# Attention steps between the products of a block-matrix layer, and an earlier first input

## The chip, the cores and the metric

The kernel runs on one core of a Trainium2 chip. The metric is device time in microseconds (us) of one execution. The engines are named as in the profile: PE (TensorE, matrix products), ACT (ScalarE), DVE (VectorE), POOL (GpSimd) and SP (SyncE, which here only issues DMAs). Each engine executes its instructions in the order in which the program writes them; they meet through semaphores.

## The reference

An attention over 4 batches, 8 heads, 768 positions and head size 64 is followed by a mixture of 4 experts over the 3072 tokens that it yields.

```python
scores = scale * np.matmul(q, k.transpose(0, 1, 3, 2))
mask = np.where(retr[0, :, 0, 0, None, None], full_mask, stream_mask)
scores = np.where(mask[None, :, :, :], scores, -1000000000.0)
...
a = a / (np.sum(a, axis=-1, keepdims=True) + 1e-09)
return np.matmul(a, v).astype(np.float32)
...
p = domain_probs / (domain_probs.sum(-1, keepdims=True) + 1e-09)
for e in range(E):
    h = np.maximum(x @ w1[e], 0.0)
    out += p[:, e:e + 1] * (h @ w2[e])
```

Three heads ("retrieval": 0, 2 and 6) attend to all earlier positions. The other five ("window" heads) see the first 4 positions and the last 64. The rows of x are the heads' outputs side by side (512 wide); w1 is 512 x 1024 and w2 1024 x 512 for each expert.

## The kernel before, in words

**Two streams in one program.** The program does not start the second half after the first. It writes attention steps between steps of the expert layers. Attention is cut into 8 groups, one for each batch and half sequence (384 query rows, all heads); group g gives three tiles of 128 tokens, `xT[g]`. The expert layers are `moe_steps` (L1163): token tiles 0 to 2 together, expert by expert (`plain_steps`, L937), then tile 3 alone, expert by expert, then ten pairs of tiles (`pair_steps`, L1046).

**A pair.** For each expert, `scale_inputs` (L1017; the DVE operation is L1028) multiplies `xT` by the routing probabilities `pB` into one of two buffers `xs`. The first layer (PE L1059) makes 4 banks of 8 matmuls for an expert, 16 banks for a pair, each emptied by one Relu of ACT (L1068) into six blocks of `hA`. PE's banks come from `bank` (L98), which has four buffers `pA` in turn; attention scores (L627) take from the same four. The second layer of all four experts together is written as seven half-size block products (PE L1092) on sums of blocks, each of 16 matmuls in two halves. ACT copies (`keep`, L1110) and DVE additions (`add`, L1113) combine the products; sums of weight blocks are made once (`weight_sums`, and `last_weight_sum`, L927), sums of input blocks while the first layer runs (`input_sums`, L1032, on DVE L1036 and L919) and between the products (`fourth_sum`, L1122).

**Shared space.** The finished sums of tiles 0 to 3 lie in `hA` too (`acc_of`, L933): tile 0's where block 3 of the pairs lies. They are stored by SP (L992) at the end of the plain steps. The Relu that writes there must wait for the store.

**A window head.** Its keys are transposed by SP from `kSr` to `kS` (L255), once a group. Its score (L627: seven matmuls of 54 or 55 columns) goes through ACT's Exp (L645) and DVE's mask (L649); the values (L739) go to one of two buffers `pV`; ACT takes the reciprocal of the row sums as Ln (L757) and Exp (L767), and DVE scales into `xT` (L762), which releases the buffer. `later` (L895) puts that DVE operation into the program only after 1300 ns of planned time (`LAG`, L893), so other DVE work may stand ahead of it. In group 2 and later the heads follow in the order 0, 2, 6, 1, 3, 5, 7, 4, so five window heads end a group. Retrieval heads use L675 for the values.

**What sets the order.** Every step of `moe_steps` yields its planned duration and a share. The main loop (L1245) sums duration times share in `spent`, and writes attention steps while the group is behind its plan: `plan[a]` (L1207) gives the value of `spent` at which group a begins and ends, and `att_ns` the group's length. `require` (L1233) writes all that is left of a group that the next step reads. POOL's loads for the next group are written when a group begins (`loads`, L1188) and behind the values.

The lines that follow are those of the profile.

The softmax here doesn't subtract the row's maximum and nothing guards it: scores larger than these inputs give would overflow.

## Time and profile before

| | |
|---|---|
| median of 13 runs | 402.8 us (400.33 to 404.1) |
| the profiled execution, its own time | 400.92 us |
| its span, first to last instruction | 399.2 us |
| PE busy | 379.7 us (95%), 3814 matmuls |
| DVE, ACT, POOL busy | 219.2, 231.2, 138.9 us |
| mean granted PE clock | 0.991 |
| pair layer 1 on PE (L1059) | 156.2 us, 1280 matmuls |
| seven products on PE (L1092) | 76.4 + 58.4 us, 640 + 480 matmuls |
| window heads on PE, first and last of group 2 | 101.99 us, 121.04 us |

Busy PE time counts overlapping matmuls, each with a modelled end, so 95% does not say how much could be saved; the waits of PE do. A wait is the idle time just before an instruction, with the engine or DMA that ended it. A timeline line reads: start, duration, engine, source line, operation, what is written from what, sizes, how many, and in brackets the idle time before it. Times count from the first instruction.

### The profile page before, as it was taken

What the parts mean: (1) busy time and instruction counts of PE and PEld (TensorE: products, weight loads), DVE (VectorE), ACT (ScalarE), POOL (GpSimd) and SP (SyncE); (2) the same over time, 40 slices, a digit from 0 to 9 for tenths busy, and PEclk for the clock granted to TensorE, in tenths of its full rate; (3) what the DMA queues carried; (4) which work ended last, traced back from release to release, by engine and by line L of the source; (5) the groups of instructions that cost most, each with busy time, mean ns of one, the idle gap of its engine ahead of it and who ended that gap; (6) DMA issues with size and microseconds to landing.
All of it is one profiled execution on the core that took longest, in us unless ns stands there. A gap on an engine that the chain in (4) does not pass through costs nothing.

```text
span 399.2 us, 9362 instructions
## 1 busy us (share of the span) xinstructions
PE 379.7 (95%) x3814; PEld 314.5 (79%) x3814; DVE 219.2 (55%) x472; ACT 231.2 (58%) x476; POOL 138.9 (35%) x182
## 2 busy tenths in 40 slices
PE   8899999996798997999999999999999999999996
PEld 4755556574687896899988898899988898888885
DVE  7736787545364465565554465574643465454440
ACT  3754469462495587375684487476683585361641
POOL 8824734973436605731454016621200000000000
PEclk9999999998899999999999999999999999999999
DMA  9999999999999999994799659993790120110101
GB/s 163 162 208 195 188 166 163 166 113 139 221 162 151 157 104 173 144 170 84 74 170 146 105 89 134 190 186 32 72 195 15 55 59 7 53 54 2 54 0 54
DMA packets 167631, 47.67 MB, mean 119 GB/s; under 512 B 156492, under 2 KB 161316, under 8 KB 167588
## 3 DMA queue, kind: packets, MB, share of 16 engines
q0 software_dynamic: 102656, 20.98, 73.3%
q1 hardware_dynamic: 63332, 25.70, 32.5%
q8 instruction: 30, 0.49, 0.5%
q10 hardware_dynamic: 1600, 0.39, 0.5%
q14 instruction: 13, 0.11, 0.1%
HBM read 48.82 MB, written 6.34 MB: 138 GB/s over the span
## 4 chain that ended last, share of the span: by engine, by line
PE 56%; ACT 3%; DVE 1%; issue 1%; ACTq 0%
PE pO L1092 26%; PE pA L1059 25%; PE pA L627 3%; ACT hA L1068 1%; PE pV L675 1%; PE pV L739 1%; ACT rc L757 1%; DVE xT L762 1%; ACT es L645 0%; DVE hA L919 0%; ACT rc L767 0%; DVE es L649 0%; DVE hA L1036 0%; ACT o L1154 0%; ACTq L1154 0%
## 5 line engine op out<-in xcount | busy, mean ns | idle before, releaser
L1059 PE MATMUL pA<-xs,w1sb 128*128 128x256 f16 x1280 | 156.2, 276 | 2.6 <-DVE xs L1028 2.6
L1059 PEld LDWEIGHTS <-w1sb 128*128 128x128 f16 x1280 | 122.6, 99 | 18.2 <-issue 2.9
L1068 ACT ACTIVATE hA<-pA 128x512 f16<-128x512 f32 x160 | 94.8, 598 | 44.5 <-PE pA L1059 35.5
L1092 PEld LDWEIGHTS <-hA 128*128 128x128 f16 x1120 | 107.1, 98 | 12.8
L645 ACT ACTIVATE es<-pA 128x384 f16<-128x384 f32 (+2 forms) x122 | 60.2, 510 | 39.1 <-PE pA L627 37.0
L1092 PE MATMUL pO<-w2sb,hA 128*128 128x256 f16 x640 | 76.4, 273 | 0.0
L281 POOL DMA_DIRECT2D vS<-in_v_dram x30 | 29.3, 983 | 89.4 <-PE pV L739 88.8
L1092 PE MATMUL pO<-tsb,hA 128*128 128x256 f16 x480 | 58.4, 273 | 0.0
L1028 DVE TENSOR_TENSOR xs<-xT,pB 128x1024 f16<-128x1024 f16 (+1 forms) x52 | 49.5, 973 | 16.0 <-PE pA L1059 15.9
L919 DVE TENSOR_TENSOR hA<-hA 128x1024 f16<-128x1024 f16 (+1 forms) x80 | 41.9, 554 | 0.9
L233 POOL DMA_DIRECT2D kSr<-in_k_dram x30 | 29.6, 998 | 19.1 <-issue 9.6
L963 ACT ACTIVATE hA<-pA 128x384 f16<-128x384 f32 (+1 forms) x64 | 22.3, 386 | 18.9 <-PE pA L950 17.8
L950 PE MATMUL pA<-xT,w1sb 128*128 128x384 f16 (+1 forms) x256 | 31.7, 273 | 0.2
L649 DVE TENSOR_TENSOR es<-es,mC 128x256 f16<-128x256 f16 (+1 forms) x42 | 10.8, 258 | 38.1 <-ACT es L645 37.8
L1113 DVE TENSOR_TENSOR o<-pO,s 128x256 f32<-128x256 f32 x30 | 12.7, 425 | 34.3 <-PE pO L1092 23.2
L971 PE MATMUL pO<-w2sb,hA 128*128 128x512 f16 x128 | 30.5, 380 | 0.3 <-DMA w2sb<-in_moe_w_dram 0.3
L649 DVE TENSOR_TENSOR es<-es,mS 128x384 f16<-128x384 f16 (+1 forms) x40 | 13.8, 348 | 30.4 <-ACT es L645 30.3
L762 DVE TENSOR_TENSOR xT<-pV,rc 64x384 f16<-64x384 f32 x37 | 20.4, 554 | 12.7 <-ACT rc L767 10.4
L757 ACT ACTIVATE rc<-pV,eps 64x384 f32<-64x384 f32 x37 | 21.3, 575 | 10.1 <-PE pV L739 9.4
L1110 ACT COPY s<-pO 128x256 f32<-128x256 f32 x30 | 11.2, 372 | 27.3 <-PE pO L1092 25.7
L950 PEld LDWEIGHTS <-w1sb 128*128 128x128 f16 x256 | 19.3, 98 | 8.5 <-issue 0.7
L627 PE MATMUL pA<-qT,kR 128*128 128x384 f16 (+2 forms) x120 | 24.6, 280 | 1.1 <-ACT hA L963 0.4
(113 smaller groups left out, 337.0 us busy)
## 6 DMA issues: line engine op xcount, KB each, us to landing
pB<-p_rows SPq DMA_DIRECT2D x10, 512.0 KB
out_dram<-o SPq DMA_DIRECT2D x19, 256.0 KB
w1sb<-in_moe_w_dram POOLq DMA_DIRECT2D x8, 512.0 KB, 9.8
w2sb<-in_moe_w_dram POOLq DMA_DIRECT2D x4, 1024.0 KB, 13.5
kSr<-in_k_dram POOLq DMA_DIRECT2D x30, 112.0 KB, 6.0
vS<-in_v_dram POOLq DMA_DIRECT2D x30, 112.0 KB, 4.6
q<-in_q_dram POOLq DMA_DIRECT2D x18, 128.0 KB, 7.6
vR<-in_v_dram POOLq DMA_DIRECT2D x24, 48.0 KB, 5.2
```

What stands on the lines that cost most here:

```text
L233: gp.dma_start(out=kSr[:, :, SH.index(h), own(h)], in_=windows_of(k, b, h, c),)
L281: gp.dma_start(out=t[:, :, own_v(h)], in_=windows_of(v, b, h, c))
L627: nc.tensor.matmul(out=ps[:, o : o + nq], lhsT=key_tile(b, c, h, t), rhs=qTs[b, c][:, hp, q0 : q0 + nq], start=(n == 0 or not first), stop ...
L645: nc.scalar.activation(out=es[:, 0:cols], in_=ps[:, 0:cols], func=AF.Exp, scale=SC)
L757: nc.scalar.activation(out=rc[r, :], in_=ps[o, 0:CH], func=AF.Ln, bias=eps[o, :])
L919: nc.vector.tensor_tensor(out=out, in0=a, in1=b, op=ALU.subtract)
L950: nc.tensor.matmul(out=pss[ft][:, 0:cols_n], lhsT=w1sb[:, e * DMP + ct, ft * P : (ft + 1) * P], rhs=x[:, ct, :], start=(n == 0), stop=(n = ...
L971: nc.tensor.matmul(out=ps_o, lhsT=hs[:, ft, j * P : (j + 1) * P], rhs=w2sb[:, e * FTP + ft, :], start=(ft == 0), stop=(ft == FTP - 1),)
L1028: nc.vector.tensor_tensor(out=o, in0=xin, in1=pb.to_broadcast([P, DMP, n, P]), op=ALU.mult)
L1059: nc.tensor.matmul(out=ps[:, f * PC : (f + 1) * PC], lhsT=w1sb[:, e * DMP + ct, (f0 + f) * P : (f0 + f + 1) * P], rhs=xs[:, ct, :], start= ...
L1068: nc.scalar.activation(out=blocks[:, b0 : b0 + 2, k0 : k0 + 2, :].rearrange("p t f x -> p f t x"), in_=ps.rearrange("p (f t x) -> p f t x" ...
L1092: nc.tensor.matmul(out=ps, lhsT=a[:, k, :], rhs=b(k), start=(first and k == 0), stop=(k == KT - 1), skip_group_check=not first,)
```

## The change

Four things change.

- In `pair_steps` a step of the first layer now counts 0.5 and a half product 1.57 in `spent`; both counted 1.0. The shares of the plain steps (0.6 and 1.4), which held only for tiles 0 to 2, now hold for tile 3 as well, since the main loop uses every step's share. So attention is written mostly between the products.
- The first scaled inputs of the first pair are written behind expert 1 of tile 3, two experts earlier than before (E is 4).
- The last weight sum of expert 3 is not written behind tile 3, but behind the first bank of the first pair.
- Group 2 ends, and group 3 begins, at 0.72 of a pair instead of 0.66.

```diff
+    PSHARE = 1.57
+
     def pair_steps(nt0, nxt):

-        sums = []
+        sums = [lambda: last_weight_sum(E - 1)] if nt0 == pair0 else []
         for e in range(E):
...
                 if sums:
                     sums.pop(0)()
-                yield 2 * DMP * mm_ns(PC), 1.0
+                yield 2 * DMP * mm_ns(PC), 0.5
...
                 if k == KT // 2 - 1:
-                    yield KT // 2 * mm_ns(HN), 1.0
+                    yield KT // 2 * mm_ns(HN), PSHARE
...
         last = nxt is None
-        half = KT // 2 * mm_ns(HN), 1.0
+        half = KT // 2 * mm_ns(HN), PSHARE
...
             yield from plain_steps(3, 1, e, lambda: xT[1][:, :, 0:P], n0)
-            last_weight_sum(e)
-            if e == E - 1:
+            if e + 1 < E:
+                last_weight_sum(e)
+            if e == E - 3:
                 scale_inputs(pairs[0], 0)
...
-    for a, n in zip(range(2, G), (0.66, 1.65, 3.2, 4.65, 6.2, 7.65)):
+    for a, n in zip(range(2, G), (0.72, 1.65, 3.2, 4.65, 6.2, 7.65)):
...
     for ns, share in moe_steps():
-        spent += ns * (share if spent < E * UNIT else 1.0)
+        spent += ns * share
```

On PE the order of the instructions changes from tile 3 on; their number and kinds do not. On DVE the `scale_inputs` of the first pair and the weight sum move as told. On SP the four stores of tiles 0 to 3 now stand together, behind the key transpose of group 2 where three of them stood before, and the loads of `pB` shift by a place against the transposes of a few groups. The lines of the changed kernel are 3 or 4 higher than before from L1046 on: L1059 becomes L1062, L1068 L1071, L1092 L1095, L1110 L1113, L1113 L1116.

## The prediction

> **What bounds the kernel now.** Read first the list of waits, TensorE alone. From 60 us on PE waits four times only, 11.3 us together:

> ```profile
> PE pV L739 <- DVE xT L762: 5.4, 6, 2.2
> PE pA L627 <- DMA kS<-kSr: 2.9, 1, 2.9
> PE pA L1059 <- DVE xs L1028: 2.6, 1, 2.6
> PE pA L627 <- ACT hA L963: 0.4, 1, 0.4
> ```

> Elsewhere it streams: 8 matmuls of 256 columns take 0.87 us wherever the chain of waits shows them alone. No matmul is removed, so the change can win at most these 11.3 us. The last three waits are neighbours, and the timeline of 90 to 104 us shows what stands behind them. TensorE:

> ```profile
> 94.32 1.03 PE L1059 MATMUL pA<-xs,w1sb 128*128 128x256 f16 x8 [2.58 <-DVE xs L1028]
> ...
> 101.99 0.47 PE L627 MATMUL pA<-qT,kS 128*128 128x54 f16 x7 [2.94 <-DMA kS<-kSr]
> 102.28 1.89 PE L1059 MATMUL pA<-xs,w1sb 128*128 128x256 f16 x8
> ```

> ScalarE, idle in the same stretch, but not waiting for PE:

> ```profile
> 97.40 0.60 ACT L1068 ACTIVATE hA<-pA 128x512 f16<-128x512 f32 x1 [1.42 <-PE pA L1059]
> 97.89 0.38 ACT L645 ACTIVATE es<-pA 128x256 f16<-128x256 f32 x1
> 102.60 0.60 ACT L1068 ACTIVATE hA<-pA 128x512 f16<-128x512 f32 x1 [4.33 <-DMA out_dram<-hA]
> ```

> The third Relu of a pair writes blocks 2 and 3 of hA, where tile 0's finished sum lies (`acc_of`), so it waits for that sum's store. The store stands in SP's queue behind the transpose of the window keys:

> ```profile
> 90.44 8.47 SPq L255 DMA_TRANSPOSE kS<-kSr  x1
> 99.00 1.49 SPq L992 DMA_DIRECT2D out_dram<-hA  x3
> ```

> So two DMAs hold this place: kS at 101.99 and the store at 102.60. And the table of windows shows the clock (columns: stretch, us, busy time and count of five engines, granted PE clock, DMA share, GB/s):

> ```profile
> 91.80:95.20 3.40, 0.88 (x9) 0.79 (x9) 3.40 (x5) 0.00 (x0) 1.03 (x2) 1.00 1.72 121
> 95.20:98.60 3.40, 3.40 (x23) 2.46 (x21) 1.12 (x5) 1.47 (x3) 0.00 (x0) 0.51 1.44 174
> 98.60:102.10 3.50, 0.56 (x8) 0.22 (x6) 0.00 (x0) 0.00 (x0) 0.00 (x0) 0.99 1.40 231
> 102.10:105.50 3.40, 3.40 (x27) 2.59 (x26) 1.26 (x5) 1.58 (x3) 3.04 (x4) 0.50 1.20 285
> ```

> Each stretch in which PE idled is followed by one at half clock: the x8 of L1059 took 1.89 at 102.28.

> **Part 1, first scaled inputs earlier, group 2 begun later.** Two L1028 of 1.2 us each (2.35 for both) leave the place before L1059. The first now stands behind last_weight_sum(1), at about 85 us, the second among group 2's masks; the last weight sum (0.68) moves behind the pair's first bank, and its reader is only the fifth product. pB, issued at 69.53, has 15 us to land; were it late, DVE's masks and evictions would queue behind the L1028, under the cover described next. The 0.42 wait goes because that score now stands four layer-2 matmuls later. So PE starts layer 1 at 91.57, when L971 ends, not at 94.32.

> Now what is late next. I count PE work D from the pair's first layer-1 matmul, at full clock: 0.87 a bank, 0.18 for six L675 or seven 54-column matmuls, 0.11 for a 256-column score. Before, the kS score stands at D = 3 x 0.87 + 0.18 + 0.11 = 2.91. After, by the new order, layer 1 issues five banks, one L675 group and one score first: D = 5 x 0.87 + 0.29 = 4.66, reached at 91.57 + 4.66 = 96.23. The next bank, the pair's sixth, is the one that the third Relu must empty (`bank` has four, and a score took one between). Nothing that the change moves is ahead of the store on SP: the transpose waits for kSr's DMA and the store for the transpose's issue. So the Relu still starts at 102.60 and ends at 103.20, and PE restarts at about 103.25 at D = 4.66. The 2.58 and 2.94 are not saved; they become **one wait of 7.0 us**, named for L1068's counterpart or the store. Behind that Relu on ACT queue two Relus and an exponential, at a pitch of 0.5 against PE's 0.87 a bank; they catch up.

> Before, PE restarts at 101.99 with D = 2.91 and does half speed until 105.49: D = 2.91 + 3.50/2 = 4.66 there. After, at 105.49: 4.66 + 2.24/2 = 5.78 if the clock comes back then, 1.12 ahead. If it stays at half one stretch more, to 108.90, D is 4.66 + 5.65/2 = 7.49 against 4.66 + 3.41 = 8.07: 0.58 behind. Which? The stretch 102.07 to 105.49 would be 2.24/3.42 = 66% busy. Stretches that were 26% and 16% busy did not keep the clock, full ones did; at the start of the kernel, PE is busy from 1.27, and the slow matmuls last until about 6.5. 66% lies between, so I take the middle, **0.27 us gained**, ends +1.12 and -0.58.

> [...]

> **Part 2, attention between the products.** In layer 1 PE waits for nothing after 106 us, so fewer attention steps there win nothing. What may win is the tails of the groups, where five window heads A to E end a group. `pV` has two buffers, so C waits until A is scaled: 0.39 from A's L739 to its end, Ln 0.58, Exp 0.52, the L762 0.56, small gaps, 0.1 to PE: 2.3 us if no engine has other work. Rows:

> ```profile
> 121.43 0.58 ACT L757 ACTIVATE rc<-pV,eps 64x384 f32<-64x384 f32 x1 [0.84 <-PE pV L739]
> 122.04 0.52 ACT L767 ACTIVATE rc<-rc 64x384 f32<-64x384 f32 x1
> ```

> Before, the tails wait 2.04 (group 2, at 121.04), 2.23 (group 3, 155.20), 0.58 (group 5, 242 to 244) and 0.59 (group 7, 331 to 333). For after I walk each tail by the new order of ACT and DVE, counting from A's start.

> Group 2: A, B, C, D, E stand at 0, 2.11, 3.34, 4.39, 5.45 of PE work. DVE: the mask of the next score ends at 2.61, then the first add of the products (its product is ready at 2.31) 2.63 to 3.05, then A's scale to 3.63: C starts at 3.78, **0.44 late**. B's scale, behind one more mask, ends at 5.08: D at 5.23, 0.40 late. L919 (0.68) goes before C's scale, which ends at 6.35: E 0.21 late. Sum 1.05, so 0.99 gained.

> Group 3: 0, 1.24, 2.47, 3.53, 3.71, closer, because the planner is behind and issues two heads at once. The mask ahead of A's scale waits for an exponential that ACT does after A's Ln and Exp (2.03): A's scale ends 2.98, C 0.66 late. ACT: B's Ln and Exp to 3.17, a copy, an exponential to 4.08; DVE's mask to 4.45, B's scale to 5.03: D 0.99 late. C's scale to 5.80: E 0.59 late. Sum 2.24: nothing gained.

> Groups 5 and 7: 0, 1.23, 3.34, 4.39, 5.45 each, and A's scale stands ahead of the add. D 0.45 to 0.5 and E 0.15 late: 0.58 and 0.65, nothing gained. Groups 4 and 6 (2 to 3 us between heads) wait in neither kernel. Tails: **0.9 us gained**; each walk may err by 0.3.

> Other queues: group 3's key transpose starts after the last kS score of group 2 (about 119 us) and takes 6.3, first use at about 145; group 4's q transposes, now behind a pB load on SP, have about 7 us of slack; POOL's vS loads follow the values, which end within a microsecond of before. All hidden.

> **Sum.** 0.27 + 0.9 = 1.2 us. The profiled execution took 400.92 (span 399.2, 1.7 around it): 399.7 after. It lies 1.9 below the median of the 13 runs, 402.8, so by the same difference **401.6**, that is 0.29% faster. With the ends of the clock and the tails: 400.3 to 402.6.

> **Rivals.**
> - The store does not hold PE (it lands earlier, or a bank is free). Then PE stops at the kS score, D = 6.40, until 101.99, and its lead is 6.40 - 2.91 = 3.49; with the tails 4.4: **398.4**. For: it is what the new order of group 2 does if only PE's own waits counted. Against: the 4.33 row of ACT and the unchanged order on SP.
> - Slower: the scale operations in groups 5 and 7 are delayed as in group 3, 2.24 each. Place: pairs 4 and 7, second to fourth product. It decides once A's scale falls behind the mask that waits for the next exponential. Price 2 x 1.66 = 3.3: **404.9**; one group alone 403.2. For: the same 1.23 from A to B as in group 3. Against: in the order, A's scale is ahead.
> - The moves do what they say and are worth nothing: that is the lower end of my sum, 402.5.

> **Chances.** Forecast 0.72, store rival 0.13, slower rival 0.15. 0.3% (1.2 us) is about what a measurement of this kernel tells from no change. The forecast lies on that bound: 0.30 of its 0.72 is faster (clock back at once, 400.7), 0.40 the same, 0.02 slower. Faster 0.43, same 0.40, slower 0.17. Range 398.0 to 404.3, from the store rival to most of the slower one.

> **What would show it.** A wait of some 7 us of PE between 96 and 103, ACT's third Relu still released by out_dram at about 102.6, no wait for xs, half clock after 103; PE's waits for L762 near 4.5 in all, over 2 of it in group 3. If that Relu runs before 100, or the L762 waits pass 6, I am wrong.

## The result, and the profile after

The changed kernel takes **397.83 us** in the median of 11 runs (396.88 to 403.18), the kernel before 403.22 us in the median of 48 (398.61 to 404.47). The ratio is **0.9894, 95% interval 0.9864 to 0.9924**: 3.1 to 5.5 us faster, 4.3 in the middle (the plain medians lie 5.4 apart; the ratio, which has the interval, is used in what follows). The forecast was 401.6, a gain of 1.2. The measured median lies just under the range's lower end of 398.0; by the ratio, from the 402.8 that the forecast started from, it would be 398.5, just inside. The profiled execution took 397.6 us (span 395.9, against 399.2), so 3.3 us of the difference can be looked up in the two traces. PE is busy 378.4 us, in the same 3814 matmuls.

First the list of waits, TensorE alone (us in total, times, the longest). From 60 us on, only these two are left:

```profile
PE pA L1062 <- ACT hA L1071: 6.6, 1, 6.6
PE pV L739 <- DVE xT L762: 2.4, 6, 0.7
```

The waits for `xs` (2.6) and `kS` (2.9) are gone, and one wait of 6.6 us has come. PE's timeline shows its place:

```profile
95.14 0.27 PE L627 MATMUL pA<-qT,kR 128*128 128x256 f16 x1
102.01 3.57 PE L1062 MATMUL pA<-xs,w1sb 128*128 128x256 f16 x16 [6.60 <-ACT hA L1071]
105.38 0.53 PE L627 MATMUL pA<-qT,kS 128*128 128x54 f16 x7
105.73 2.92 PE L1062 MATMUL pA<-xs,w1sb 128*128 128x256 f16 x16
```

ScalarE's timeline, where the third Relu of the pair is the first of three, and the SP queue's:

```profile
101.36 1.57 ACT L1071 ACTIVATE hA<-pA 128x512 f16<-128x512 f32 x3 [8.23 <-DMA out_dram<-hA]
```

```profile
90.98 6.89 SPq L255 DMA_TRANSPOSE kS<-kSr  x1
97.97 2.01 SPq L992 DMA_DIRECT2D out_dram<-hA  x4
```

The store of tile 0's sum is issued behind the key transpose, the Relu waits for the store, and PE, with all four banks full, waits for the Relu. When the `kS` score comes, at 105.38, there is no wait for the keys any more. The 16 matmuls after the wait take 3.57 us, twice the usual 1.91, because the clock is at half for three stretches (columns as in the table of windows before):

```profile
97.57:100.98 3.41, 0.00 (x0) 0.00 (x0) 0.00 (x0) 0.00 (x0) 0.00 (x0) 0.50 1.37 263
100.98:104.39 3.41, 2.38 (x12) 1.65 (x12) 0.23 (x1) 2.33 (x5) 3.21 (x4) 0.50 1.05 252
104.39:107.81 3.42, 3.42 (x23) 2.49 (x22) 0.52 (x2) 1.26 (x4) 1.72 (x2) 0.50 1.84 156
```

PE works at half speed from 102.01 to 107.81, which costs 5.80/2 = 2.9 us; before, it was 1.75.

The tails of the groups. PE's timeline of `pV`, groups 2 and 3; groups 5 and 7 have one wait of 0.28 each:

```profile
122.27 0.35 PE L739 MATMUL pV<-es,vS 128*128 128x54 f16 x7 [0.37 <-DVE xT L762]
154.59 0.36 PE L739 MATMUL pV<-es,vS 128*128 128x54 f16 x7 [0.35 <-DVE xT L762]
156.53 0.36 PE L739 MATMUL pV<-es,vS 128*128 128x54 f16 x7 [0.72 <-DVE xT L762]
157.33 0.36 PE L739 MATMUL pV<-es,vS 128*128 128x54 f16 x7 [0.44 <-DVE xT L762]
```

**The account, profile against profile.** The tails cost 2.44 instead of 5.4: 3.0 gained. At the start of the pair, take the time at which PE restarts, add what the half clock costs after it, and subtract the work D that it had already done (D as in the prediction): before 101.99 + 1.75 - 2.91 = 100.83, after 102.01 + 2.90 - 4.66 = 100.25. That is 0.6 gained. But the Relu ran at 101.36 here and not at 102.60, since the key transpose's issue took 6.89 us instead of 8.47; with the store as late as before, and the clock as long at half after it, this place would have lost 0.7 (an estimate). Together 3.6, against 3.3 in the spans. (The 0.3 too many comes from the way the list measures a wait; measured from start to start, as told further down, the tails gain 2.7, and the sum is 3.3.)

So the tails pay, and the front turns two waits into one. That is theory T; its rival F says that the earlier first inputs pay. The runs below test it. The first four were timed beside the kernel before on one chip (median 403.36), the last four on another (403.12).

### The profile page after: what moved, and what is told of

Read it like the earlier page. It is cut to its first block, busy times and chain, and to the rows that moved or that the text cites. A ratio compares the mean times of both kernels' runs of the same rounds, so it can differ in the third digit from the quotient of the medians.

```text
span 395.9 us, 9358 instructions
## 1 busy us (share of the span) xinstructions
PE 378.4 (96%) x3814; PEld 314.0 (79%) x3814; DVE 219.2 (55%) x472; ACT 233.8 (59%) x476; POOL 140.0 (35%) x182
## 4 chain that ended last, share of the span: by engine, by line
PE 82%; DMA 7%; ACT 4%; POOL 3%; DVE 2%; issue 1%; SPq 1%; POOLq 0%; ACTq 0%
PE pA L1062 36%; PE pO L1095 28%; DMA w2sb<-in_moe_w_dram 7%; PE pO L971 5%; PE pA L627 5%; PE pA L950 4%; PE pV L675 2%; PE pV L739 2%; ACT es L645 1%; ACT rc L757 1%; POOL vS L285 1%; DMA out_dram<-hA 1%; DVE xT L762 1%; ACT rc L767 1%; SPq L255 1%
## 5 line engine op out<-in xcount | busy, mean ns | idle before, releaser
L1062 PE MATMUL pA<-xs,w1sb 128*128 128x256 f16 x1280 | 149.5, 276 | 6.6 <-ACT hA L1071 6.6
L1062 PEld LDWEIGHTS <-w1sb 128*128 128x128 f16 x1280 | 124.6, 99 | 22.5 <-issue 6.8
L1071 ACT ACTIVATE hA<-pA 128x512 f16<-128x512 f32 x160 | 94.8, 597 | 50.3 <-PE pA L1062 39.7
L1095 PEld LDWEIGHTS <-hA 128*128 128x128 f16 x1120 | 105.7, 98 | 12.5
L1095 PE MATMUL pO<-w2sb,hA 128*128 128x256 f16 x640 | 79.0, 273 | 0.0
L645 ACT ACTIVATE es<-pA 128x384 f16<-128x384 f32 (+2 forms) x122 | 59.9, 511 | 32.0 <-PE pA L627 29.3
L1028 DVE TENSOR_TENSOR xs<-xT,pB 128x1024 f16<-128x1024 f16 (+1 forms) x52 | 49.7, 975 | 24.1 <-PE pA L1062 23.8
L1095 PE MATMUL pO<-tsb,hA 128*128 128x256 f16 x480 | 59.8, 273 | 0.0
L919 DVE TENSOR_TENSOR hA<-hA 128x1024 f16<-128x1024 f16 (+1 forms) x80 | 41.5, 553 | 1.0
L963 ACT ACTIVATE hA<-pA 128x384 f16<-128x384 f32 (+1 forms) x64 | 22.2, 386 | 18.7 <-PE pA L950 17.8
L971 PE MATMUL pO<-w2sb,hA 128*128 128x512 f16 x128 | 30.7, 380 | 0.1
L1113 ACT COPY s<-pO 128x256 f32<-128x256 f32 x30 | 11.2, 372 | 25.5 <-PE pO L1095 23.6
L950 PEld LDWEIGHTS <-w1sb 128*128 128x128 f16 x256 | 19.2, 98 | 8.3 <-issue 0.5
L762 DVE TENSOR_TENSOR xT<-pV,rc 64x384 f16<-64x384 f32 x37 | 20.4, 554 | 9.0 <-ACT rc L767 6.8
L627 PE MATMUL pA<-qT,kR 128*128 128x384 f16 (+2 forms) x120 | 24.0, 278 | 0.9 <-ACT qT L538 0.4
L1036 DVE TENSOR_TENSOR hA<-hA 128x512 f16<-128x512 f16 (+1 forms) x30 | 15.3, 511 | 16.9 <-ACT hA L1071 16.7
L757 ACT ACTIVATE rc<-pV,eps 64x384 f32<-64x384 f32 x37 | 21.3, 575 | 4.4 <-PE pV L739 3.7
```

The costliest lines, as they stand in the source:

```text
L627: nc.tensor.matmul(out=ps[:, o : o + nq], lhsT=key_tile(b, c, h, t), rhs=qTs[b, c][:, hp, q0 : q0 + nq], start=(n == 0 or not first), stop ...
L645: nc.scalar.activation(out=es[:, 0:cols], in_=ps[:, 0:cols], func=AF.Exp, scale=SC)
L757: nc.scalar.activation(out=rc[r, :], in_=ps[o, 0:CH], func=AF.Ln, bias=eps[o, :])
L919: nc.vector.tensor_tensor(out=out, in0=a, in1=b, op=ALU.subtract)
L950: nc.tensor.matmul(out=pss[ft][:, 0:cols_n], lhsT=w1sb[:, e * DMP + ct, ft * P : (ft + 1) * P], rhs=x[:, ct, :], start=(n == 0), stop=(n = ...
L971: nc.tensor.matmul(out=ps_o, lhsT=hs[:, ft, j * P : (j + 1) * P], rhs=w2sb[:, e * FTP + ft, :], start=(ft == 0), stop=(ft == FTP - 1),)
```

## The experiments

**between_only.** The new shares apply in the pairs alone; first inputs, weight sum, tile 3 and group 2's end are as before.

```diff
-        sums = [lambda: last_weight_sum(E - 1)] if nt0 == pair0 else []
+        sums = []
...
-            if e + 1 < E:
-                last_weight_sum(e)
-            if e == E - 3:
+            last_weight_sum(e)
+            if e == E - 1:
...
-    for a, n in zip(range(2, G), (0.72, 1.65, 3.2, 4.65, 6.2, 7.65)):
+    for a, n in zip(range(2, G), (0.66, 1.65, 3.2, 4.65, 6.2, 7.65)):
...
-        spent += ns * share
+        spent += ns * (share if spent < E * UNIT or spent >= first_pair else 1.0)
```

> The shares of the pairs alone (0.5 in the first layer, 1.57 between the products); first scaled inputs, last weight sum, start of group 2 and the shares of tile 3 as before. Theory T (the gain comes from the tails of the groups, where window heads wait for DVE's L762; the early edits only turn two waits into one): about 3 us faster than before, ratio 0.990 to 0.994; PE waits for L762 fall from 5.4 to about 2.5, the wait for xs (2.6) and that for kS (about 3) stay. Rival F (the gain comes from the first scaled inputs being ready earlier): ratio 0.998 to 1.002.

Measured: 400.43 us, ratio 0.9907 (0.9877 to 0.9937). The three largest of PE's waits from 60 us on (the others come to 1.5):

```profile
PE pA L627 <- DMA kS<-kSr: 5.3, 1, 5.3
PE pV L739 <- DVE xT L762: 2.8, 2, 1.9
PE pA L1062 <- DVE xs L1028: 2.6, 1, 2.6
```

The shares alone carry most of the gain, with both front waits still there: T. The tails go from 5.4 to 2.8; the ratio says 3.7 us, so about one more is not in this list. In this one execution the keys landed late (5.3 against 2.9 before and about 3 expected) and the clock was at half from 100.85 to 111.09 (mean granted clock 0.987; the 23 matmuls from 105.27 took 5.07), so its span, 399.4, shows none of the gain; only the medians do.

**front_only.** The other way round: PSHARE and the first layer's share go back to 1.0.

```diff
-    PSHARE = 1.57
+    PSHARE = 1.0
...
-                yield 2 * DMP * mm_ns(PC), 0.5
+                yield 2 * DMP * mm_ns(PC), 1.0
```

> The other edits alone: first scaled inputs two experts earlier, last weight sum later, group 2 at 0.72, shares of tile 3; pairs count 1.0 everywhere. T: ratio 0.996 to 1.001, one PE wait of 4 to 7 us that ends with the third Relu or the kS score at about 102, none for xs, and about 5 us of waits for L762. F: ratio about 0.990, 4 us faster.

Measured: 402.12 us, ratio 0.9968 (0.9942 to 0.9993). Its two largest waits (one of 0.4 is left):

```profile
PE pA L627 <- DMA kS<-kSr: 7.8, 1, 7.8
PE pV L739 <- DVE xT L762: 3.8, 7, 2.1
```

The front edits alone gain 1.3 us (0.3 to 2.3), about a third of the whole. The tails were expected to wait about 5 us and wait 3.8, 1.6 less than before, since moving group 2 takes nearly all of its own tail wait (0.18 is left of 2.04). That is as much as the whole gain, so the list leaves none of it to the earlier inputs. The `xs` wait of 2.6 is gone and the wait for `kS` has become 7.8: the same work meets the same transpose. This speaks against F.

**late_first_inputs.** The changed kernel, with only the first scaled inputs back at their old place.

```diff
-            if e == E - 3:
+            if e == E - 1:
```

> The changed kernel with the first scaled inputs back behind expert 3 of tile 3, all else as changed. T: within 0.8 us of the changed kernel (ratio to before 0.988 to 0.992): a PE wait for xs of about 2.6 us appears and the wait for the third Relu shrinks by as much, PE resumes at the same 101 to 103 us. F: 2 to 3 us slower than the changed kernel, ratio 0.995 to 1.0.

Measured: 397.66 us, ratio 0.9868 (0.9822 to 0.9915), a little under the range expected. The three largest waits:

```profile
PE pA L1062 <- DVE xs L1028: 2.1, 1, 2.1
PE pV L739 <- DVE xT L762: 2.0, 5, 0.7
PE pA L1062 <- ACT hA L1071: 1.9, 1, 1.9
```

Undoing the early inputs loses nothing measurable: F falls. The one long wait is two short ones again, and the third Relu still starts only at 103.00, released by the store:

```profile
103.00 1.57 ACT L1071 ACTIVATE hA<-pA 128x512 f16<-128x512 f32 x3 [4.56 <-DMA out_dram<-hA]
```

**sums_moved.** Is it the store? Here the sums of tiles 0 to 3 lie in blocks of `hA` that the pairs write later (and tile 3's own blocks in their place); no instruction is added, dropped or moved against the changed kernel.

```diff
-        n0 = 2 * FTP * CH + nt * 2 * DM if nt < 3 else 6 * KT * P - 2 * DM
+        n0 = 4 * KT * P + nt * 2 * DM
...
-            n0 = 2 * FTP * CH + 3 * 2 * DM + (e % 2) * FTP * P
+            n0 = 2 * FTP * CH + (e % 2) * FTP * P
```

> The changed kernel with the sums of tiles 0 to 3 in blocks 4 and 5 of hA, and tile 3's hidden rows in block 3, so that no Relu writes where a sum waits for its store. Same instructions in the same order. T: the third Relu runs at about 94 us, PE goes on to the kS score (1.74 us of work further) and waits there until kS lands at 101 to 102, 4 to 5 us instead of 6.6; 1.5 to 2.5 us faster than the changed kernel, ratio to before 0.983 to 0.987. Rival S (the store does not hold PE, kS alone does): same time as the changed kernel, within 0.5 us.

Measured: 393.65 us, ratio 0.9753 (0.9713 to 0.9793): by the ratios 5.7 us faster than the changed kernel, where 1.5 to 2.5 were expected. PE's timeline:

```profile
96.65 1.91 PE L1062 MATMUL pA<-xs,w1sb 128*128 128x256 f16 x16
102.59 0.41 PE L627 MATMUL pA<-qT,kS 128*128 128x54 f16 x7 [4.03 <-DMA kS<-kSr]
```

The wait for the Relu is gone. PE does two more banks and then meets the keys, the next thing late: a wait of 4.0, followed by one stretch at half clock instead of three in all. So the store was the hold, and a shorter wait saves twice, in itself (6.6 to 4.0) and in the clock (2.9 to 1.7). These two come to 3.8 us; what gave the rest is not shown.

**before_sums_moved.** The same move of the sums in the kernel before.

> The kernel before with the sums of tiles 0 to 3 in blocks 4 and 5 and tile 3's hidden rows in block 3. Theory T (in the kernel before the kS score ends PE's wait and the store lands behind that wait's cover): ratio 0.997 to 1.002. Rival S2 (the store costs time in the kernel before as well): ratio 0.985 to 0.993, as much as it gave behind the change.

Measured: 403.35 us, ratio 1.0011 (0.9979 to 1.0043). The store costs nothing measurable there, where the keys hold PE at D = 2.91, ahead of the bank that the Relu must free. It costs only behind the change, which lets PE reach that bank first.

**after_again.** The changed kernel once more, timed beside before_sums_moved and the next two.

> The changed kernel once more, beside the others of this set. Ratio to before 0.987 to 0.992; PE waits 5 to 8 us for the third Relu, and half clock lasts until 4 to 7 us after it.

Measured: 399.05 us, ratio 0.9884 (0.9842 to 0.9925). Its wait for the Relu was 7.7, PE restarted at 103.79, and the clock was at half from 99.39 to 109.63.

**fill.** What does the clock cost in that wait? 55 matmuls of 256 columns, whose result nobody reads, stand ahead of the bank that PE waits for. The lines are 7 higher.

```diff
+                if (nt0, e, f0) == (pair0, 1, 2):
+                    idle = pO.tile([P, DM], FP32, name="pO", bufs=2)
+                    for _ in range(55):
+                        nc.tensor.matmul(
+                            out=idle[:, 0:PC], lhsT=w1sb[:, 0, 0:P], rhs=xs[:, 0, :],
+                            start=True, stop=True,
+                        )
```

> The changed kernel with 55 matmuls of 256 columns, whose result nobody reads, ahead of the pair's sixth bank, where PE waits for the third Relu: 6.0 us of work in a wait of 6.6. Theory C (the long wait costs once more through the clock, 2.9 us in the changed kernel's profile): clock 1.00 after the wait and 1.5 to 3 us faster than the changed kernel. Rival (the half clock after the wait costs nothing, since other engines bound that stretch): within 0.7 us of the changed kernel; if the wait is shorter than 6 us in most executions: slower by the rest, up to 2 us.

Measured: 396.75 us, ratio 0.9835 (0.9802 to 0.9869). The interval overlaps that of after_again, but the two traces can be laid side by side. PE's timeline of fill:

```profile
95.71 6.17 PE L1063 MATMUL pO<-xs,w1sb 128*128 128x256 f16 x55
104.00 1.91 PE L1069 MATMUL pA<-xs,w1sb 128*128 128x256 f16 x16 [2.12 <-ACT hA L1078]
```

and of after_again:

```profile
103.79 3.57 PE L1062 MATMUL pA<-xs,w1sb 128*128 128x256 f16 x16 [7.72 <-ACT hA L1071]
```

PE restarts at the same time, 104.00 and 103.79, and the next 16 matmuls take 1.91 instead of 3.57. The mean granted clock is 1.000 against 0.987, the span 395.1 against 397.7: 2.6 us less, which is nearly all the clock's, and near the 2.9 that the account gives.

**sums_moved_later_keys.** The wait for the keys that sums_moved left, attacked too: group 2 is spread over the later part of its first stretch, so that its first `kS` score comes later.

```diff
-    begin = E * UNIT + 0.6 * ONE
-    for a, n in zip(range(2, G), (0.72, 1.65, 3.2, 4.65, 6.2, 7.65)):
+    begin = E * UNIT + 0.8 * ONE
+    for a, n in zip(range(2, G), (0.8, 1.65, 3.2, 4.65, 6.2, 7.65)):
```

> sums_moved, and group 2 begun at 0.8 of tile 3 and ended at 0.8 of a pair (0.6 and 0.72 in the changed kernel), so that the first kS score stands at 11.1 us of PE work into the first pair instead of 6.4. Theory: kS lands 10 to 10.5 us after the pair begins, so its wait of 4.0 goes, and the half clock behind it: 3 to 5 us faster than sums_moved, ratio to before 0.963 to 0.969. Rival (DVE, held by the stores at the first input sums, takes its place as what PE waits for): within 1 us of sums_moved.

Measured: **391.33 us, ratio 0.9704 (0.9661 to 0.9748)**, the fastest version run. By the ratios that is 2.0 us faster than sums_moved, with overlapping intervals, where 3 to 5 were expected. (The two profiled spans differ by 4.5, but the profiled run of sums_moved was the slowest of its six.) PE's timeline at the first `kS` score:

```profile
102.40 0.37 PE L627 MATMUL pA<-qT,kS 128*128 128x54 f16 x7 [0.73 <-ACT hA L1071]
```

The wait of 4.0 has become one of 0.73, no longer for the keys. The remaining waits from 60 us on are those of the tails, 2.5, and one of 0.3. In this profile the clock was at 1.00 in all of 98.50 to 108.70; its mean over the span of 389.2, 0.996, leaves about one half stretch elsewhere (0.004 x 389.2 = 1.6 us lost, an estimate).

## Why the prediction was right, and where it was off

**Right: the front.** One wait in place of two, its cause and its length: 7.0 forecast, 6.6 and 7.7 measured. The Relu is still released by the store, the `xs` wait and the 0.42 wait are gone, and PE began the pair at 90.59 (forecast 91.57). That the length came so near is in part luck: PE reached its stop about 1 us earlier than forecast, and the Relu ran 1.2 us earlier, so the two errors offset each other. The store stood behind the transpose on SP as before, and sums_moved shows that it was the hold. The store rival (398.4) gives nearly the measured time, but its mechanism fell: PE stopped for the store, as the sum said. So the range reaches the measured time by luck: its lower end, 398.0, was set by that rival, while the sum's own ends, 400.3 to 402.6, miss 398.5. The rival of slower tails fell too: groups 5 and 7 wait 0.28 each, not 2.24.

**Off: the term for the tails, 0.9 forecast and 3.0 measured.** This is the step that moved the sum. By group the listed waits are 0.37 (forecast 1.05), 1.51 (2.24), 0.28 (0.58) and 0.28 (0.65). Two causes.

First, the term set two measures against each other. The waits before, 5.4 in all, are idle time counted from the recorded end of the matmuls ahead; my walks counted from start to start. PE's timeline before, group 3:

```profile
151.93 1.03 PE L1092 MATMUL pO<-w2sb,hA 128*128 128x256 f16 x8
155.20 0.36 PE L739 MATMUL pV<-es,vS 128*128 128x54 f16 x7 [2.23 <-DVE xT L762]
```

and after, just ahead of the wait at 154.59:

```profile
153.88 0.36 PE L627 MATMUL pA<-qT,kS 128*128 128x54 f16 x7
```

Where PE does not wait, the next group starts 0.87 behind the start of eight such matmuls and 0.20 behind seven of 54 columns, though they are recorded for 1.03 and 0.36. So the head here lost 155.20 - 151.93 - 0.87 = 2.40 us before and 154.59 - 153.88 - 0.20 = 0.51 after, where the list has 2.23 and 0.35. Counted in this way for every head, the tails lose 6.4 us before and 3.7 after, a gain of 2.7; and the walks' 4.5 (1.05, 2.24, 0.58 and 0.65) would have forecast a gain of 1.9, not 0.9.

Second, every walk was still too long: counted so, the groups lose 0.74, 2.00, 0.47 and 0.48. The errors, 0.1 to 0.3, are about within my bound of 0.3 for each; but all lie on the same side, and the range had room for them only as if they could cancel. DVE's timeline in group 3 shows why:

```profile
153.62 0.36 DVE L649 TENSOR_TENSOR es<-es,mS 128x384 f16<-128x384 f16 x1 [1.45 <-ACT es L645]
153.90 0.54 DVE L762 TENSOR_TENSOR xT<-pV,rc 64x384 f16<-64x384 f32 x1
154.36 0.68 DVE L919 TENSOR_TENSOR hA<-hA 128x1024 f16<-128x1024 f16 x1
```

The scale starts at 153.90, though the mask before it is recorded until 153.62 + 0.36 = 153.98, and the next operation starts 0.08 before the scale's end. The walk added such durations end to end; in these rows the queued operations overlap by 0.08 each, so the chain goes by the distances between starts.

**Off: the clock.** Between "back at 105.49" and "one more half stretch" I took the middle, +0.27. It was the second: after the restart the clock stayed at half for 5.8 us, the loss of 2.9 that stood behind my lower end of -0.58. With the store at its old time this place would by the account's estimate have lost 0.7, near that end. A stretch that was 66% busy by estimate, 2.38 of 3.41 us in the trace, ran at half and was followed by another at half.

**What stays open.** The gain is 4.3 us by the ratio (3.1 to 5.5), and 3.3 in the two profiles, which the tails (2.7) and the front (0.6) explain. The remaining microsecond is within the interval. One candidate is on record: a tail's wait can also cost clock. In before_sums_moved, whose tails are those of the kernel before, the wait of 2.04 us in group 2 was followed by half clock (columns as above):

```profile
119.83:123.24 3.41, 1.37 (x19) 1.11 (x18) 2.22 (x5) 2.46 (x6) 0.52 (x1) 1.00 1.51 104
123.24:126.65 3.41, 3.41 (x19) 2.38 (x17) 1.55 (x4) 0.94 (x2) 3.41 (x5) 0.50 1.29 146
```

Such a stretch costs 3.41/2 = 1.7 us. In the profile of the kernel before, the stretches with the waits of 2.04 and 2.23 (119.14 to 122.56, 153.28 to 156.69) were 44% busy and the clock stayed at 1.00; in that of the changed kernel the stretches with the longest waits of groups 2 and 3 (121.46 to 124.88, 155.60 to 159.01) were 89% and 66% busy, and it stayed as well. How often each happens in executions without a profile is not shown.

## What to carry to other kernels

Taking away a wait of the bounding engine gains only up to the next thing that is late: here two waits of 2.6 and 2.9 became one of about 7, because a store queued behind a transpose had been hidden by them, and moving a buffer (no instruction more or less) was then worth more than the whole change. Add a chain of queued operations by the distances between their starts in the trace, not by their durations, compare waits only when both are measured in the same way, and expect the errors of like chains to add up. Before timing the cure of a wait on PE, count what the clock adds: in the changed kernel 2.6 to 2.9 us on a wait of about 7.

## What the runs showed of the hardware

  | clock of the stretch | next at half: PE busy (run, start) | next at full: PE busy (run, start) |
  |---|---|---|
  | full | 5% (sums_moved, 99.36), 14% (before, 98.66), 27% (before, 91.84), 37% (after, 94.16; late_first_inputs, 92.91), 40% (before_sums_moved, 119.83) | 44% (before, 119.14 and 153.28), 58% (late_first_inputs, 99.73), 66% (after, 155.60), 77% (sums_moved, 95.95) |
  | half | 0% (after, 97.57), 15% (front_only, 99.88), 70% (after, 100.98) | 95% (front_only, 103.29), 100% (before, 95.25 and 102.08; after, 104.39; late_first_inputs, 96.32; sums_moved, 102.77) |

- **The same transpose took 5.86 to 9.87 us to issue** in ten executions of these kernels (`kS` from `kSr`, group 2), and the third Relu was released 3.4 us after the first of the stores was issued in one execution (after) and 8.4 in another (late_first_inputs). What sets these is not settled; the spread of 4.0 us is as large as the effect of most edits here, so single profiles of the front are compared with care.
